# Float32 scores for items 8 to 15, a third VectorE pass for w1 and w2, and a DMA for q's second copy

## The chip, the cores and the metric

The kernel runs on one core of a Trainium2 chip. The metric is the device time of one execution in microseconds, lower is better. The engines named below are TensorE (PE; PEld is its weight load), VectorE (DVE), ScalarE (ACT), GpSimd (POOL) and SyncE (SP), which here issues all DMAs.

## The reference

Three stages run one after the other on 4 x 576 = 2304 tokens: an attention with 32 heads of 64, causal, whose scores have a decay added; a gated block (two products multiplied, then w3 and w_out); and a soft mixture of 8 experts with 4 slots each. What matters here:

```python
scores = scale * np.matmul(q, k.transpose(0, 1, 3, 2))
bias = -(cum[:, :, :, None] - cum[:, :, None, :])        # cum: running sum of max(s, 0)
scores = np.where(causal, -1000000000.0, scores + np.minimum(bias, 0.0))
...
attn = attn / (np.sum(attn, axis=-1, keepdims=True) + 1e-09)
x = attn @ v
a = x @ w1
b = x @ w2
h = a * b @ w3
x = h @ w_out
```

w1, w2, w3 and w_out reach the kernel as 64-bit floating point words, which it turns into float32 itself.

## The kernel before

**Items.** The attention is cut into 40 items (ITEMS). Items 0 to 7 are heads 0 to 7 with query tiles 0 to 2 (320 queries); items 8 to 15 are the same heads with tiles 3 and 4 (256 queries against 448 and 576 keys); items 16 to 39 are heads 8 to 31 with all five tiles. A step of the loop in att_steps does, for item n, its scores (att_scores), the scaling of item n-1 by its row sums (att_norm), the preparation of item n+1 (att_prep), the fetch of item n+2 (att_fetch), the transposes of item n-1 (att_transpose) and, for every second n, the product with v (att_pv).

**Scores, two ways.** Items below NF32 (8 before) multiply float32 operands: the raw tile holds q and k on 64 partitions and the decay rows on four more, and L323 multiplies 68 partitions of it; each such product is two TensorE instructions. Later items take float32r operands: the raw tile is fetched with q and k on both halves of the partitions (128), VectorE rounds q and k into qa (L295, L298), q's rounded copy goes into qb (L297, on ScalarE for n < 24 and on VectorE after), GpSimd subtracts to get the remainder of k in qb (L299) and of q in qa (L302), and L323 makes two products, with qa (128 partitions) and with qb (68).

**Tiles.** raw, qa and qb have two buffers each. A raw tile is free for the next fetch when its last reader is done: the casts and subtractions for a float32r item, the score matmuls themselves for a float32 item.

**Weights.** w1 and w2 come as 16 pieces of 512 words (k = 0 to 15 in load_words). convert makes float32 of one: ScalarE scales the high word (L182) and turns the low word into its shifted integer (L185); VectorE shifts and joins (L186) and puts the sign in (L189). Then ScalarE rounds it into the stationary operand (L205) and GpSimd subtracts to get the remainder (L206). w3 and w_out go through convert too, in two layouts.

**Order.** SP's instructions (all DMA issues) run in the order of the program. The other engines are ordered by a planner with its own costs, from the dependencies and the order of the program. The program weaves the attention's steps, the gated block's halves (glu_half, L421) and the pieces of weights by hand (weave): pieces 0 to 7 go with the first nine items, pieces 8 to 15 and the first gated halves with the items after that, and later pieces of w3 and w_out with the rest.

Of the kernel before, what the change touches and what calls it, by code (L numbers as in the profile page):

```python
# [10 lines left out]
F32 = mybir.dt.float32  # L11
F32R = mybir.dt.float32r
I32 = mybir.dt.int32
U32 = mybir.dt.uint32
I64 = mybir.dt.int64
AF = mybir.ActivationFunctionType
ALU = mybir.AluOpType
# [30 lines left out]
def attn_glu_softmoe_kernel(  # L48
# [14 lines left out]
    nc = tc.nc  # L63
# [19 lines left out]

    NW, NRAW, NG4, NX, NE_ = 8, 3, 4, 6, 11
    NRW, SCB, PTB, QAB, VB = 2, 3, 2, 2, 2
    NF32, NDIR, ND = 8, 2, 1

    A1, CA, CB1, CB, GB1, GB, GC = 0.6, 8, 16, 26, 8, 16, 24

# [84 lines left out]
        nc.sync.dma_start(raw, {"w12": w12, "wo": wo, "w3": w3, "wot": wot, "w3t": w3t}[kind][i, :, 512 * e : 512 * e + 512])  # L174
        words[k] = raw

    def convert(k, w):
        raw = words.pop(k)
        pair = raw.bitcast(I32).rearrange("p (n t) -> p n t", t=2)
        hi, lo = pair[:, :, 1], pair[:, :, 0]  # L180
        wi, wu = w.bitcast(I32), w.bitcast(U32)
        nc.scalar.activation(out=w, in_=hi.bitcast(F32), func=AF.Copy, scale=F64_SCALE)  # L182

        lu = lo.bitcast(U32)
        nc.scalar.activation(out=lo, in_=lu, func=AF.Copy, scale=LO_SCALE, bias=-0.49999)  # L185
        nc.vector.scalar_tensor_tensor(  # L186
            out=wi, in0=wi, scalar=3, in1=lo, op0=ALU.logical_shift_left, op1=ALU.bitwise_or
        )
        return nc.vector.scalar_tensor_tensor(  # L189
            out=wi, in0=hi, scalar=-0x80000000, in1=wi, op0=ALU.bitwise_and, op1=ALU.bitwise_or  # L190
        )

    w12_t = [None] * FC
    rows_t, rows_w = {}, {}

    def load_words(k, ap):
        (kind, i), e = TODO[k // 2], k % 2
        span = slice(512 * e, 512 * e + 512)
        if kind == "w12":
            if e == 0:  # L200
                w12_t[i] = wp.tile([P, 2, 2, KC, P], F32R, tag="W", name=f"w12t_{i}", bufs=NW)
            w = gq.tile([P, 512], F32, tag="g4", name=f"w_{kind}_{i}_{e}", bufs=NG4)
            convert(k, w)
            th, tl = (w12_t[i][:, n].rearrange("p a k f -> p (a k f)")[:, span] for n in range(2))
            nc.scalar.copy(out=th, in_=w)  # L205
            nc.gpsimd.tensor_tensor(out=tl, in0=w, in1=th.bitcast(F32), op=ALU.subtract)  # L206
        elif k < 2 * N0:
            if e == 0:
                rows_t[kind, i] = gq.tile([P, FC, P], F32, tag="g4", name=f"{kind}_{i}", bufs=NG4)
            rows_w[kind, i] = convert(k, rows_t[kind, i].rearrange("p c f -> p (c f)")[:, span])  # L210
        else:
            if e == 0:
                rows_t[kind, i] = ap.tile([P, 1024], F32, tag="words", name=f"w_{kind}_{i}", bufs=NRAW)
            w = rows_t[kind, i]
            convert(k, w[:, span])
            if e == 1:
                nc.sync.dma_start({"wo": wo_d, "w3": w3_d}[kind][i], w)

# [53 lines left out]
    def att_prep(n, ap):  # L272
        h, tiles = ITEMS[n]
        t = hd[n]
        raw, q0, q1 = t["raw"], t["q0"], t["q1"]
        if h % 2:
            vt = ap.tile([P, 9, 2, D], F32, tag="v", name=f"v_{n}", bufs=VB)
            nv = 2 * tiles[-1] + 1
            nc.sync.dma_start(vt[:, :nv], v[h // 2, :, :nv])
            t["v"] = hd[n - 1]["v"] = vt  # L280
        if n < NF32:
            rows = raw
        else:
            rows = ap.tile([P, 2, S], F32R, tag="qb", name=f"qb_{n}", bufs=QAB)
            qa = ap.tile([P, 2, S], F32R, tag="qa", name=f"qa_{n}", bufs=QAB)
        if n < NDIR:
            for a in range(2):
                nc.sync.dma_start(rows[64 + 2 * a : 66 + 2 * a, :, :q1].bitcast(F32), dec[a][h : h + 1, :, :, :q1])
        else:
            nc.sync.dma_start(rows[64:68, :, :q1].bitcast(F32), rows_d[h].rearrange("a b n t -> (a b) n t")[:, :, :q1])  # L290
        if n < NF32:
            t["mul"] = [rows[:68]]
            return
        rq, rk, qb = raw[:, 0], raw[:, 1], rows
        nc.vector.tensor_copy(qa[:, 0, q0:q1], rq[:, q0:q1])  # L295

        (nc.scalar.copy if n < 24 else nc.vector.tensor_copy)(qb[0:64, 0, q0:q1], rq[0:64, q0:q1])  # L297
        nc.vector.tensor_copy(qa[:, 1, :q1], rk[:, :q1])  # L298
        nc.gpsimd.tensor_tensor(  # L299
            out=qb[0:64, 1, :q1], in0=rk[0:64, :q1], in1=qa[0:64, 1, :q1].bitcast(F32), op=ALU.subtract  # L300
        )
        nc.gpsimd.tensor_tensor(  # L302
            out=qa[64:, 0, q0:q1], in0=rq[64:, q0:q1], in1=qa[64:, 0, q0:q1].bitcast(F32), op=ALU.subtract
        )
        t["mul"] = [qa, qb[:68]]
# [314 lines left out]
    def att_steps(ap):  # L620

        groups = [[] for _ in range(B + 1)]
        N = len(ITEMS)
        for n in range(N + 1):
            tiles = ITEMS[n][1] if n < N else ()
            old = [i for i in ITEMS[n - 1][1] if i] if 0 < n <= N else []
            sc = [(0.2 + 0.3 * i, lambda i=i, n=n: att_scores(n, i, ap)) for i in tiles]
            tr = [(0.2 + 0.3 * i, lambda i=i, n=n: att_transpose(n - 1, i, ap)) for i in old]
            norm = [(0, lambda n=n: att_norm(n - 1))] if 0 < n <= N else []
            prep = [(0, lambda n=n: att_prep(n + 1, ap))] if n + 1 < N else []  # L630
            if n + 2 < N:
                prep += [(0, lambda n=n: att_fetch(n + 2, ap))]
            blks = [k for k in range(2) if BLK[k][2][0] in ITEMS[n - 1][1]]
            pv = [(1.4, lambda n=n, k=k: att_pv(n - 2, k)) for k in blks] if n > 0 and n % 2 == 0 else []
            groups[min(B, max(0, (n - 1) // H))] += [
                *sc[:1], *norm, *sc[1:2], *prep, *sc[2:3], *tr[:1], *sc[3:4], *tr[1:2], *sc[4:], *tr[2:], *pv
            ]
        return groups
# [78 lines left out]
    with tc.tile_pool(name="att", bufs=1) as ap:  # L717
# [11 lines left out]
            out=mask[:, S - P :], in_=mask[:, S - P :], pattern=[[-1, P]], base=0,  # L729
# [4 lines left out]
        att = att_steps(ap)  # L734
        decay_rows()
        att_prep(0, ap)
        for k in range(2, NRAW):
            fetch_words(k, ap)
# [13 lines left out]
        def load(k):  # L752
            i = k // 2 - 1
            if FC <= i < N0:
                (sum_rows if k % 2 else use_rows)(*TODO[i])
            if k < 2 * N0:
                load_words(k, ap)
            if k + NRAW < 2 * N0:
                fetch_words(k + NRAW, ap)

        def load_later(i):
            for e in range(2):
                fetch_words(2 * i + e, ap)
            for e in range(2):
                load_words(2 * i + e, ap)
# [10 lines left out]
        k = GC - GB  # L776
        steps = steps[GB:]
        run(weave(att[2], weave(steps[:k], prep[CB:]) + steps[k:]))
        for b in range(2, B):
            steps, late = glu_steps(b - 1, late)  # L780
            n = len(more) // (B - b)
# [70 lines left out]
    for a in range(0, 4, 2):  # L852
        zt_ps = psum("tp", f"zt_ps_{a}")
        for c in range(2):
            nc.tensor.transpose(zt_ps[:, c * P : (c + 1) * P], z_acc[:, (a + c) * P : (a + c + 1) * P], ident)
        nc.vector.tensor_reduce(
            out=zt[:, a : a + 2], in_=zt_ps[:, : 2 * P].rearrange("p (c t s) -> p c s t", t=2, s=2 * NS),
# [14 lines left out]
    for q in range(4):  # L872
        cols = slice(256 * q, 256 * q + 256)
        yps = psum(("acc", "sg")[q % 2], f"y_ps_{q}")
        for r in range(2):
            for j in range(4):
                f = 4 * r + j
# [10 lines left out]
    for r in range(2):  # L888
        for c in range(2):
            for j in range(4):  # L890
                f = 4 * r + j
# [94 lines left out]
    for c in range(2):  # L986
# [10 lines left out]
        for n in CH[c]:  # L997
            ot = big(OT[n_out], f"ot_{n_out}").rearrange("p (n d) -> p n d", d=256)[:, : 2 * n]
            for m in range(n):
                op = psum("sg", f"out_ps_{n_out}_{m}")  # L1000
                for e in range(2):
# [7 lines left out]
                    out=ot[:, 2 * m : 2 * m + 2].rearrange("p n d -> p (n d)"), in_=op  # L1009
# [54 lines left out]
```

## Time and profile before

| | us |
|---|---|
| median of 3 runs | 590.42 |
| lowest and highest | 587.47, 592.25 |
| profiled execution | 585.76 |
| its span, first to last instruction | 583.9 |
| TensorE busy in it | 527.3 |
| VectorE, ScalarE, GpSimd busy in it | 347.9, 323.8, 218.6 |

An engine's busy time is the time in which an instruction of it was under way; matmuls are pipelined and their ends are modelled, so a busy TensorE is not one at its peak. A profile tells for each group of instructions how long one takes, how long the engine stood idle before them, and what ended that idle time. The granted clock is the share of its full speed that TensorE was given.

### The profile page before, as it was taken

To read this page: it belongs to the slowest core of one execution; us is meant where nothing else is said; L and a number is where in the kernel's file an instruction comes from. 1 tells how busy PE (TensorE), PEld (TensorE's weight loads), DVE (VectorE), ACT (ScalarE), POOL (GpSimd) and SP (SyncE) were. 2 spreads that over 40 slices of the span, in tenths; PEclk is the share of its full clock that TensorE was granted. 3 is DMA by queue.
4 is the path that set the end of the run, shared out by engine and by line. 5 is a ranking of instruction groups with operands and counts; after the bars stand their busy time and mean duration, and the time that the engine had idled before them with its cause. 6 is when DMAs were issued, how large, how long until landed. Compare 5 with 4: busy or idle time off the path is not lost. (4 is left out here: it accounts for less than half of the span.)

```text
span 583.9 us, 11901 instructions
## 1 busy us (share of the span) xinstructions
PE 527.3 (90%) x4324; PEld 443.6 (76%) x4324; DVE 347.9 (60%) x989; ACT 323.8 (55%) x877; POOL 218.6 (37%) x260
## 2 busy tenths in 40 slices
PE   1878988998698999989999889999999999999994
PEld 1655967787587797978989779898988999843463
DVE  6548998698887477484686756566740311252532
ACT  5767876778767666655566557466833321321212
POOL 5447887445927445161364443523410000001000
PEclk9995889998989999989999999999999999999999
DMA  6556744777562333524545254464450996689947
GB/s 200 178 164 192 241 153 174 245 273 262 188 196 81 126 101 122 165 79 156 182 160 174 92 172 139 128 211 172 134 222 32 375 407 244 238 305 421 419 175 262
DMA packets 37881, 116.19 MB, mean 199 GB/s; under 512 B 3808, under 2 KB 10656, under 8 KB 34368
## 3 DMA queue, kind: packets, MB, share of 16 engines
q1 hardware_dynamic: 37824, 115.45, 56.4%
q8 instruction: 34, 0.56, 0.4%
q14 instruction: 23, 0.19, 0.1%
HBM read 103.81 MB, written 11.60 MB: 198 GB/s over the span
## 5 line engine op out<-in xcount | busy, mean ns | idle before, releaser
L421 PE MATMUL gl<-x,w12t 128*128 128x320 f32 (+1 forms) x1536 | 237.0, 304 | 7.7 <-DVE nmax L326 5.6
L421 PEld LDWEIGHTS gl<-x,w12t 128*128 128x128 f32 x1536 | 214.0, 192 | 16.0 <-DVE nmax L326 7.6
L344 POOL TENSOR_SCALAR sc<-sc,rinv 128x64 f32<-128x64 f32 (+4 forms) x160 | 93.5, 603 | 68.0 <-DVE rinv L341 46.6
L331 ACT ACTIVATE sc<-sc,nmax 128x64 f32<-128x64 f32 (+4 forms) x160 | 89.5, 561 | 48.2 <-DVE nmax L326 47.8
L302 POOL TENSOR_TENSOR qa<-raw,qa 64x576 fp32r<-64x576 f32 (+1 forms) x32 | 43.5, 1358 | 135.3 <-DVE qa L295 116.6
L326 DVE CUSTOM_DVE_ANT_0 sc<-sc_ps,mask 128x64 f32<-128x64 f32 (+4 forms) x160 | 64.6, 422 | 27.9 <-PE sc_ps L323 26.0
L359 PE MATMUL pt_ps<-ident,sc 128*128 128x128 f32 x320 | 57.9, 291 | 5.6 <-ACT pt L361 2.6
L361 ACT COPY pt<-pt_ps 128x128 f32<-128x128 f32 (+3 forms) x128 | 52.0, 422 | 16.9 <-PE pt_ps L359 10.1
L323 PE MATMUL sc_ps<-qa 128*128 128x448 f32 (+1 forms) x168 | 55.5, 347 | 4.3 <-DVE nmax L326 1.8
L323 PE MATMUL sc_ps<-qb 68*128 68x448 f32 (+1 forms) x168 | 51.0, 325 | 7.9 <-DMA qb<-rows_d 7.9
L299 POOL TENSOR_TENSOR qb<-raw,qa 64x576 fp32r<-64x576 f32 x32 | 52.8, 1651 | 4.8 <-issue 0.9
L359 PEld LDWEIGHTS pt_ps<-ident,sc 128*128 128x128 f32 x320 | 38.6, 146 | 18.4 <-issue 10.4
L110 PE MATMUL x_ps<-pt,v 128*64 128x256 f32 (+1 forms) x384 | 48.4, 368 | 0.1
L427 ACT COPY a<-gl 128x256 f32<-128x256 f32 (+1 forms) x64 | 25.5, 398 | 37.8 <-PE gl L421 35.5
L964 POOL MEMSET ht<- 128x1024 f32 x2 | 1.9, 954 | 107.4 <-DVE ew L867 99.0
L186 DVE SCALAR_TENSOR_TENSOR w_w<-w_w,raw_w 128x512 int32<-128x512 int32 x32 | 25.2, 787 | 26.5 <-ACT raw_w L185 26.0
L323 PEld LDWEIGHTS sc_ps<-qb 68*128 68x128 f32 x168 | 32.8, 201 | 8.9 <-issue 8.5
L323 PEld LDWEIGHTS sc_ps<-qa 128*128 128x128 f32 x168 | 32.9, 198 | 8.4 <-DVE nmax L326 3.0
L110 PEld LDWEIGHTS x_ps<-pt,v 128*64 128x64 f32 x384 | 33.8, 146 | 6.7 <-issue 1.3
L182 ACT ACTIVATE w_w<-raw_w 128x512 f32<-128x512 f32 x32 | 21.6, 675 | 24.4 <-DMA raw_w<-in_w 24.3
L594 ACT COPY gn<-gn_ps 128x512 f32<-128x512 f32 x40 | 22.7, 584 | 18.0 <-PE gn_ps L591 17.0
L409 DVE TENSOR_TENSOR x<-x_ps,x 128x320 fp32r<-128x320 f32 (+1 forms) x32 | 13.7, 448 | 29.4 <-ACT x L408 29.4
(181 smaller groups left out, 830.2 us busy)
## 6 DMA issues: line engine op xcount, KB each, us to landing
ew<-in_ew SPq DMA_DIRECT2D x27, 1024.0 KB
raw_w<-in_w SPq DMA_DIRECT2D x32, 512.0 KB
raw<-in_qk SPq DMA_DIRECT2D x24, 576.0 KB
v<-in_v SPq DMA_DIRECT2D x16, 576.0 KB
raw_w3t<-in_w3t SPq DMA_DIRECT2D x16, 512.0 KB
raw_wot<-in_wot SPq DMA_DIRECT2D x8, 512.0 KB
raw_wo<-in_wo SPq DMA_DIRECT2D x8, 512.0 KB
w_d<-w_w SPq DMA_DIRECT2D x8, 512.0 KB
```

The costliest lines, as they stand in the source:

```text
L110: mm = nc.tensor.matmul(out_, lhs, rhs, start=start, stop=stop)
L186: nc.vector.scalar_tensor_tensor(out=wi, in0=wi, scalar=3, in1=lo, op0=ALU.logical_shift_left, op1=ALU.bitwise_or)
L299: nc.gpsimd.tensor_tensor(out=qb[0:64, 1, :q1], in0=rk[0:64, :q1], in1=qa[0:64, 1, :q1].bitcast(F32), op=ALU.subtract)
L302: nc.gpsimd.tensor_tensor(out=qa[64:, 0, q0:q1], in0=rq[64:, q0:q1], in1=qa[64:, 0, q0:q1].bitcast(F32), op=ALU.subtract)
L323: nc.tensor.matmul(pp[:r, : z - a], x[:, 0, q0 : q0 + r], x[:, 1, a:z], start=x is mul[0], stop=x is mul[-1])
L326: nc.vector.tensor_tensor_reduce(out=sc[:r, a:z], in0=pp[:r, : z - a], in1=hd["mask"][:r, m0 : m0 + z - a], scale=-0.125, scalar=3.0e38 if ...
L331: nc.scalar.activation(out=sc[:r, :W], in_=sc[:r, :W], func=AF.Exp, bias=nmax[:r, i : i + 1], scale=-1.0, accum_out=rsum[:r, i : i + 1],)
L344: nc.gpsimd.tensor_scalar(out=sc, in0=sc, scalar1=rinv[:, i : i + 1], scalar2=1.0, op0=ALU.mult, op1=ALU.mult)
L359: nc.tensor.transpose(tp[:, j * P : (j + 1) * P], sc[:, j * P : (j + 1) * P], ident)
L361: t["turned", i] = nc.scalar.copy(out=pt[:, p0 : p0 + step * (i - 1) + 1 : step], in_=tp[:, : i * P].rearrange("p (j q) -> p j q", q=P))
L421: nc.tensor.matmul(acc[:, :nt], w12_t[fc][:, wi, n, kc], x_t[b, blk, kc][:, xi], start=k == 0, stop=k == 3 * KC - 1)
L427: nc.scalar.copy(out=a_sb[:, :nt], in_=acc[:, :nt])
```

## The change

Three edits. NF32 goes from 8 to 16, so items 8 to 15 fetch q and k on 64 partitions only, have no qa and qb, and their decay rows go into the raw tile. For w1 and w2 convert leaves the low word to VectorE: it shifts the scaled high word (one tensor operand), joins the sign, and joins the low word shifted right by 29; ScalarE's pass over the low word is gone there, and w3 and w_out keep it. For items 16 to 39 q's second copy is a DMA from qa to qb inside SBUF, issued by ScalarE after VectorE's rounding, in place of a cast from raw.

```diff
-    NF32, NDIR, ND = 8, 2, 1
+    NF32, NDIR, ND = 16, 2, 1
...
-    def convert(k, w):
+    def convert(k, w, by_act):
...
         nc.scalar.activation(out=w, in_=hi.bitcast(F32), func=AF.Copy, scale=F64_SCALE)
-
         lu = lo.bitcast(U32)
+        if not by_act:
+            nc.vector.tensor_scalar(out=wi, in0=wi, scalar1=3, scalar2=None, op0=ALU.logical_shift_left)
+            nc.vector.scalar_tensor_tensor(
+                out=wi, in0=hi, scalar=-0x80000000, in1=wi, op0=ALU.bitwise_and, op1=ALU.bitwise_or
+            )
+            return nc.vector.scalar_tensor_tensor(
+                out=wu, in0=lu, scalar=29, in1=wu, op0=ALU.logical_shift_right, op1=ALU.bitwise_or
+            )
+
         nc.scalar.activation(out=lo, in_=lu, func=AF.Copy, scale=LO_SCALE, bias=-0.49999)
...
-            convert(k, w)
+            convert(k, w, False)
...
-            rows_w[kind, i] = convert(k, rows_t[kind, i].rearrange("p c f -> p (c f)")[:, span])
+            rows_w[kind, i] = convert(k, rows_t[kind, i].rearrange("p c f -> p (c f)")[:, span], True)
...
-            convert(k, w[:, span])
+            convert(k, w[:, span], True)
...
-        (nc.scalar.copy if n < 24 else nc.vector.tensor_copy)(qb[0:64, 0, q0:q1], rq[0:64, q0:q1])
+        nc.scalar.dma_start(qb[0:64, 0, q0:q1].bitcast(F32), qa[0:64, 0, q0:q1].bitcast(F32))
```

## Rows read from the trace of the kernel before

**Rows 1.** Stretches: length, busy us of PE, PEld, DVE, ACT, POOL, clock, DMA, GB/s.

```profile
36.00:47.40 11.40, 7.84 (x47) 5.26 (x47) 6.07 (x25) 7.41 (x23) 2.54 (x5) 0.77 0.74 227
47.40:63.00 15.60, 14.10 (x69) 10.92 (x69) 14.02 (x29) 11.21 (x34) 14.41 (x15) 0.51 0.72 232
63.00:97.30 34.30, 29.38 (x205) 26.68 (x201) 30.41 (x63) 26.36 (x61) 28.33 (x26) 0.95 0.56 191
...
140.00:200.00 60.00, 49.84 (x451) 43.27 (x452) 47.99 (x127) 42.92 (x119) 35.17 (x38) 0.91 0.52 176
200.00:440.00 240.00, 232.30 (x1941) 210.46 (x1940) 152.74 (x457) 145.70 (x414) 95.45 (x121) 0.99 0.44 148
```

**Rows 2.** Groups from 47 to 97 us: busy, mean ns, idle before.

```profile
L299 POOL TENSOR_TENSOR qb<-raw,qa 64x576 fp32r<-64x576 f32 x7 | 11.2, 1602 | 1.4 <-DMA raw_w<-in_w 0.5 <-PE pt_ps L359 0.5 <-ACT raw_w L185 0.4
L189 DVE SCALAR_TENSOR_TENSOR w_w<-raw_w,w_w 128x512 int32<-128x512 int32 x8 | 9.7, 1217 | 0.0
```

**Rows 3.** Single lines: count, shortest/median/longest ns, first and last start.

```profile
L185 ACT ACTIVATE raw_w<-raw_w x32: 637/661/737, 5.2 to 424.2; 128x512 int32<-128x512 uint32 x32
L186 DVE SCALAR_TENSOR_TENSOR w_w<-w_w,raw_w x32: 673/692/1900, 7.0 to 425.3; 128x512 int32<-128x512 int32 x32
L298 DVE CAST qa<-raw x32: 441/453/1684, 47.5 to 405.7; 128x576 fp32r<-128x576 f32 x32
L297 ACT CAST qb<-raw x16: 387/538/680, 47.4 to 182.3; 64x256 fp32r<-64x256 f32 x8, 64x576 fp32r<-64x576 f32 x8
L297 DVE CAST qb<-raw x16: 446/1670/1705, 196.4 to 406.1; 64x576 fp32r<-64x576 f32 x16
```

**Rows 4.** TensorE's groups by shape, 47.4 to 63 and 63 to 97.3 us.

```profile
L359 PE MATMUL pt_ps<-ident,sc 128*128 128x128 f32 x8 | 2.9, 436 | 1.1 <-ACT ptd L375 1.1
...
L421 PE MATMUL gl<-x,w12t 128*128 128x320 f32 x99 | 17.9, 333 | 4.9 <-DVE nmax L326 4.9
```

**Rows 5.** Timeline near 30 us: start, us, engine, instruction, idle before.

```profile
29.40 0.66 ACT L185 ACTIVATE raw_w<-raw_w 128x512 int32<-128x512 uint32 x1
...
30.30 0.37 PE L110 MATMUL x_ps<-ptd,v 128*64 128x64 f32 x1 [0.85 <-ACT ptd L375]
```

**Rows 6.** Timeline of TensorE's scores, with float32 (raw) and float32r (qa, qb).

```profile
35.83 1.32 PE L323 MATMUL sc_ps<-raw 68*128 68x64 f32 x6 [0.25 <-issue]
...
43.45 2.47 PE L323 MATMUL sc_ps<-raw 68*128 68x64 f32 x6 [0.47 <-DMA raw<-rows_d]
...
49.61 1.22 PE L323 MATMUL sc_ps<-qa 128*128 128x448 f32 x3 [1.32 <-POOL qa L302]
...
80.73 0.29 PE L323 MATMUL sc_ps<-qa 128*128 128x288 f32 x1
...
81.14 0.30 PE L323 MATMUL sc_ps<-qb 68*128 68x288 f32 x1
...
87.89 0.50 PE L323 MATMUL sc_ps<-qa 128*128 128x448 f32 x2
```

**Rows 7.** Timeline of a small transfer and its reader; SP's issues of L290, shortest/median/longest.

```profile
6.37 1.58 SPq L288 DMA_DIRECT2D raw<-rows  x2
...
9.22 2.47 PE L323 MATMUL sc_ps<-raw 68*128 68x64 f32 x6 [9.22 <-DMA raw<-rows]
...
L290 SPq DMA_DIRECT2D qb<-rows_d x32: 267/327/742, 42.0 to 405.2; - x32
```

**Rows 8.** Timeline of item 16: cast, second subtraction, first reduction.

```profile
108.87 0.46 DVE L295 CAST qa<-raw 128x576 fp32r<-128x576 f32 x1 [1.90 <-DMA raw<-in_qk]
...
111.06 1.42 POOL L299 TENSOR_TENSOR qb<-raw,qa 64x576 fp32r<-64x576 f32 x1
...
118.55 0.23 DVE L326 CUSTOM_DVE_ANT_0 sc<-sc_ps,mask 128x64 f32<-128x64 f32 x1 [0.30 <-PE sc_ps L323]
```

**Rows 9.** TensorE's waits, 200 to 440 us: us in total, times, longest.

```profile
PE lg L110 <- DVE nmax L326: 2.1, 1, 2.1
```

**Rows 10.** What ended ScalarE's idle time before L297: us, times.

```profile
  DMA raw<-in_qk: 5.0, 4
```

## The prediction

> **What bounds the kernel now.** I read the page's busy shares and its row of clocks first, then a table of stretches, then the groups of instructions inside the stretch that the change touches, and last the waits of each engine.
>
> The table of stretches splits the kernel into three [rows 1]. From 200 to 440 us TensorE is busy 232.3 of 240 us and nothing else comes near: the stretch is TensorE's, and what VectorE or ScalarE saves there is worth only the little that TensorE waits for them. From 140 to 200 us no engine is full: TensorE is busy 49.8 of 60. The stretch from 36 to 97.3 us is where items 8 to 15 have their scores. There three engines are nearly full together: from 47.4 to 63 us TensorE 14.1, VectorE 14.0 and GpSimd 14.4 of 15.6 us, and TensorE is granted 0.51 of its clock, which is its lower level, 1.2 GHz, for nearly all of it. From 63 to 97.3 us they are busy 29.4, 30.4 and 28.3 of 34.3 us.
>
> The groups inside this stretch show that VectorE's load is partly not its own [rows 2]: the second bitwise pass over a word takes 1.22 us on average here while GpSimd runs 1.60 us subtractions beside it, and the first pass, of the same shape, has a median of 0.69 over the kernel [rows 3]. TensorE's own idle time is 4.9 us for VectorE's score reduction and 1.1 for a ScalarE copy [rows 4].
>
> **Part by part.** The sum is made against the profiled execution (span 583.9 us, time 585.76, so 1.9 us lie outside the span). The runs shown have their median 4.7 us higher, at 590.42; I carry the difference over unchanged.
>
> *w1 and w2, words 0 to 7 (before 47 us).* ScalarE loses one 0.66 us pass for each word [rows 3], VectorE gains a shift. The trace has no integer shift with one tensor operand. Its bounds are the plain cast of 128x576, 0.45 us, and the two-operand pass of the same shape, 0.69; a shift has one tensor operand like the cast, so I take 0.45. What the ScalarE pass is worth is seen at 29.4 us: it runs, the copy of ptd starts only behind it, and TensorE waits 0.85 us for that copy [rows 5]. If all eight passes stood so, 8 x 0.66 = 5.3 us would come back; if all eight shifts stood on the path, 8 x 0.69 = 5.5 us would be lost. VectorE is the emptier of the two here, busy 6.1 of 11.4 us against ScalarE's 7.4 from 36 us on [rows 1]. I take -1.0 us.
>
> *Items 8 to 15 and words 8 to 15 (36 to 97.3 us).* Taken away for each item: VectorE's two casts, ScalarE's cast, and GpSimd's two subtractions, of which the long one alone is 1.60 us [rows 2]. TensorE pays. Six instructions over 576 columns of float32 operands took 1.32 us behind other matmuls and 2.47 us at 43.45 us, after gaps [rows 6]; the two are a factor of 1.9 apart, as the two levels of the clock are. Per column that is 2.29 and 4.29 ns, so an item of 448 + 576 columns costs 2.35 or 4.39 us. The float32r items cost, at the higher level, 0.71 us for the four matmuls of 288 columns (80.73 to 81.44) and 0.50 for the two of 448, together 1.21; at the lower, 1.22 for the three with qa and as much again for the same columns with qb, 2.44 us [rows 6]. The difference is +1.14 us or +1.95 us for an item. With three items at the lower level (8 to 10, before 63 us) and five at the higher: 3 x 1.95 + 5 x 1.14 = 11.6 us; bounds 9.1 and 15.6.
>
> The Trainium skill, "FP8 and Floating Point Precision", TensorE Precision Notes, says that true FP32 takes four passes through the array. As an estimate by that page, at 2.4 GHz against two single passes, an item would cost 0.85 us more and all eight 6.8; the rows say 9.1 at that level, and the sum goes by the rows.
>
> What comes back: item 8's scores start at 49.61 us, when GpSimd's result is there, though item 7's ended at 43.45 + 2.47 = 45.92, so 3.7 us; the 4.9 us and 1.1 us of [rows 4]; the lower clock from 63 us on, 5% of 34.3 = 1.7 us; and the gated products that follow item 7 come about 3.2 us earlier, since items 8 and 9 no longer put their two 1.60 us subtractions in front of item 7's scaling on GpSimd, and with them the higher clock, which is worth half, 1.6. That is 13.0 us against 11.6, so -1.4 us. Bounds: +11.6 if nothing comes back. At the other end TensorE's lost capacity from 36 to 97.3 us is 3.6 + 1.5 + 4.9 us idle and 2.6 + 7.6 + 1.7 us at the lower level [rows 1], 21.9 us, less 9.1: -12.8.
>
> Where cover is needed: a float32 item reads its raw tile directly, so the fetch of the item after next waits on SP for TensorE's scores and no longer for GpSimd, and behind it on SP stand the weight words, v and the decay rows. The tile is needed two items later, and eight items fill the 50 us from 47.4 to 97.3, so two take 12 us, against 4.4 us of scores and about 3 of landing [rows 6, 7]; I cost it at nothing. If this cover goes, each fetch costs what its landing takes, about 3 us. The fetch also halves (64 partitions), which helps. VectorE's eight added shifts (8 x 0.45 = 3.6 us) take the place of its eight casts of k (0.45 us plain, [rows 3]), so the casts of q and ScalarE's eight passes over the low word are the gain.
>
> *q's copy, items 16 to 23 (97 to 200 us).* ScalarE's cast (0.68 us at the longest, [rows 3]) becomes a DMA that it issues. The trace has no copy inside SBUF; the nearest row is a small transfer: issued at 6.37, awaited by TensorE until 9.22, 2.85 us [rows 7]. It starts when VectorE's cast is done: for item 16 at 109.33, so it lands at about 112.5 with 0.33 us for the issue (SP's median for a transfer of this kind, [rows 7]), and GpSimd's second subtraction, needed by the same matmuls, ends at 112.48. VectorE's first reduction of item 16 starts at 118.55, so some 6 us cover both [rows 8]. 0 us; bounds -5.4 (8 x 0.68, all of ScalarE's cast on the path) and +2.6 (8 x 0.33). Without the cover it would be 2.85 us for an item.
>
> *q's copy, items 24 to 39 (200 to 440 us).* VectorE loses 16 casts with a median of 1.67 us, though the shortest took 0.45 [rows 3]. TensorE waits for VectorE in five rows here, 2.1 us the largest and 3.9 in all [rows 9]. I take half, -2.0 us; bounds -3.9 and +5.3 (16 issues of 0.33 us on ScalarE).
>
> Sum: -1.0 - 1.4 + 0 - 2.0 = -4.4 us: 581.4 for an execution like the profiled one, 586.0 at the median.
>
> **The rivals.**
>
> *The relief carries.* TensorE closes most of its gaps from 36 to 97.3 us and stays at the higher clock. For it: VectorE and GpSimd are both above 85% there and both are cut. Against: TensorE is as full. Near -10 us in that stretch (the bound is -12.8), -1 and -3 around it, is 14 less than the median: 576 us.
>
> *The hold passes on.* VectorE's long casts are long because GpSimd is working beside them: 0.45 us at the shortest, 1.67 at the median [rows 3]. If the next VectorE instruction is held in the cast's place, nothing is won from 200 us on, and half of the 4.9 us stays in the middle: -1.0 + (2.4 - 1.4) + 0 + 0 = 0, so 590 us. The Trainium skill, "SBUF — State Buffer", Who interferes with whom, says just this: a VectorE copy, or an operation with two SBUF inputs, and GpSimd lock each other out of a shared port pair for a whole instruction. The bitwise passes at 1.22 us agree.
>
> *ScalarE's queue is held (slower).* An issue waits for VectorE's cast, and in order behind it on ScalarE stand exp, the copies of pt, ptd and of the gate, for which TensorE waits. Before, ScalarE's cast waited only for the raw data, and even so 5.0 us over four of sixteen [rows 10]; from item 24 on ScalarE had no such wait. At 0.33 us of issue and 0.4 of hold, the 16 items from 24 on cost 11.7 us if TensorE gets all of it: 590.4 - 4.4 + 11.7 = 598 us. It decides, that is, brings the time above 590.4, from 4.4 / 16 = 0.28 us for each of them on, and makes it slower by 1% at 0.64. Against it: ScalarE is busy 145.7 of 240 us there, so a hold can be hidden.
>
> **How the numbers follow.** Forecast 0.40 (580 to 592), relief carries 0.17, hold passes on 0.17, queue held 0.26. A measurement of this kernel can tell about 1% from no change: below 584.5 is faster, above 596.3 slower. Faster: 0.17 and 0.18 of the forecast's, 0.35. Same: 0.22 of the forecast's and 0.15 of the third, 0.37. Slower: 0.26 and 0.02, 0.28. The range of 576 to 600 leaves out about half of the carried relief (0.08), a third of the held queue (0.08) and the ends of unknown costs (0.04).
>
> **What would show it.** Item 8's scores near 46 us and without a GpSimd wait; eight float32 items at 2.4 us, at most three of them at 4.4; items 8 to 15 ending between 93 and 99 us; no row of a pass over w1 or w2 at 0.66 us more on ScalarE, and a VectorE shift near 0.45; ScalarE's idle time in front of the copies' issues below 0.3 us each; TensorE's idle time from 200 to 440 us two us shorter. I am wrong if the lower clock lasts beyond 63 us (each further us costs half of one), if the float32 items come closer together than TensorE can take them, or if the planner, which orders all engines but SP by its own costs, puts the work from 97 us on in a worse order.

## The result, and the profile after

The changed kernel takes 579.4 us in the median of four runs (577.37 to 580.04); the kernel before, run beside it, 588.94 (587.31 to 592.25). The ratio is 0.9875, with a 95% interval of 0.9837 to 0.9912: faster, clear of noise though by less than 2%, by 9.5 us in the medians and 7.4 by the ratio. Here and below the medians are over all runs, the ratios and their intervals over the fast ones alone (up to 1.5% above the kernel's fastest), so the two need not agree. The time is inside the range of 576 to 600 and below the 584.5 that the prediction put as the edge of "faster", an outcome it gave 0.35; the forecast of 586.0 was 6.6 us too high, of which 1.5 lie in the baseline (588.94 here, 590.42 there). Against the baseline of its own comparison the forecast was a ratio of 0.9925 (586.0 / 590.42). The largest term of its sum, -2.0 us for q's copy from 200 us on, is not where the gain is.

The profiled execution has a span of 576.9 us (before 583.9). Its stretches, as [rows 1] (stretch and length, busy us of PE, PEld, DVE, ACT and POOL with counts, granted clock, DMA share, GB/s):

```profile
36.00:47.40 11.40, 9.55 (x71) 7.29 (x72) 7.58 (x30) 8.35 (x28) 3.42 (x5) 0.91 0.70 218
47.40:63.00 15.60, 15.01 (x59) 10.69 (x58) 13.30 (x34) 10.88 (x27) 10.81 (x13) 0.63 0.62 203
63.00:97.30 34.30, 33.22 (x234) 26.68 (x231) 24.29 (x63) 22.80 (x55) 13.19 (x15) 1.00 0.64 205
97.30:140.00 42.70, 36.29 (x270) 30.35 (x268) 33.46 (x73) 26.57 (x65) 16.53 (x16) 0.88 0.68 217
140.00:200.00 60.00, 55.49 (x522) 47.34 (x521) 46.50 (x130) 44.52 (x130) 39.56 (x43) 0.97 0.55 175
200.00:440.00 240.00, 233.87 (x1956) 212.89 (x1955) 141.47 (x436) 143.99 (x405) 89.64 (x115) 0.99 0.49 158
```

From 36 to 47.4 us TensorE is busy 9.55 us where it was 7.84. From 63 to 97.3 us it is busy 33.22 of 34.3 us (29.38) at a granted clock of 1.00 (0.95), while VectorE has fallen from 30.41 to 24.29 and GpSimd from 28.33 to 13.19. Up to 97.3 us TensorE has run 364 matmuls in these rows, 71 + 59 + 234, against 321 in the three of before. From 97.3 to 140 us it falls back: 36.29 us busy at a granted clock of 0.88, where the kernel before has, in a stretch that [rows 1] leave out:

```profile
97.30:140.00 42.70, 39.43 (x342) 33.20 (x340) 33.99 (x85) 31.47 (x79) 21.10 (x19) 1.00 0.67 225
```

From 140 to 200 us TensorE goes from 49.84 to 55.49, and from 200 to 440 us from 232.30 to 233.87.

TensorE's timeline of the changed kernel, scores of items 8, 9 and 13 from float32 operands (start, us, count last):

```profile
46.65 3.78 PE L330 MATMUL sc_ps<-raw 68*128 68x448 f32 x6
...
52.81 3.69 PE L330 MATMUL sc_ps<-raw 68*128 68x448 f32 x6
...
84.91 1.89 PE L330 MATMUL sc_ps<-raw 68*128 68x448 f32 x6
```

TensorE's waits in the changed kernel from 36 to 97.3 us (us in total, times, longest):

```profile
PE sc_ps L330 <- DVE w_w L189: 1.2, 1, 1.2
...
PE pt_ps L366 <- ACT ptd L382: 0.6, 1, 0.6
PE gl L428 <- DVE nmax L333: 0.3, 1, 0.3
```

The 4.9 us for VectorE's reduction of [rows 4] are down to 0.3, and GpSimd's 1.3 us in front of item 8 [rows 6] are gone.

The other place that changed is near 155 us. TensorE's largest wait there in the kernel before, from 140 to 200 us:

```profile
PE sc_ps L323 <- DMA qb<-rows_d: 7.1, 2, 5.8
```

SP's timeline there, also before (start, us, issues):

```profile
142.40 12.54 SPq L174 DMA_DIRECT2D raw_w3t<-in_w3t  x4
154.99 0.33 SPq L290 DMA_DIRECT2D qb<-rows_d  x1
```

The decay rows of an item stood on SP behind four pieces of w3, whose buffers VectorE had not freed, and TensorE stood idle for 5.8 us. The changed kernel has no wait for decay rows there. Following the gated products (L421 before, L428 after), the 97th starts at 95.1 us before and 94.8 after, the 241st at 150.7 and 154.3, the 289th at 184.0 and 178.4, the last at 510.9 and 503.8: by this mark no lead at 97 us, a lead of 5.6 at 184, and 7.1 at the end.

The mark follows one kind of product, and the order among the kinds changed too. By 97.3 us both kernels have begun 90 score matmuls, but of all others the changed kernel has begun 343 and the kernel before 298: 22 more products with v, 12 more transposes, 8 more products with w_out and 3 more gated ones. At the median distances between starts of such matmuls in these traces that is some 3.6 us of TensorE's time, an estimate. So there is a lead at 97 us; in these two executions it is lost by 140 us (579 others begun, 604 before), over a stretch in which the changed kernel has the lower clock, and is there again at 184 (903 and 845).

### The profile page after: what moved, and what is told of

Read it like the earlier page. It is cut to its first block, busy times and chain, and to the rows that moved or that the text cites. A ratio compares the mean times of both kernels' runs of the same rounds, so it can differ in the third digit from the quotient of the medians.

```text
span 576.9 us, 11909 instructions
## 1 busy us (share of the span) xinstructions
PE 529.7 (92%) x4324; PEld 442.1 (77%) x4324; DVE 329.8 (57%) x973; ACT 311.1 (54%) x845; POOL 195.5 (34%) x244
## 5 line engine op out<-in xcount | busy, mean ns | idle before, releaser
L428 PE MATMUL gl<-x,w12t 128*128 128x320 f32 (+1 forms) x1536 | 241.7, 308 | 3.9 <-DVE nmax L333 2.0
L428 PEld LDWEIGHTS gl<-x,w12t 128*128 128x128 f32 x1536 | 216.2, 194 | 12.6 <-DVE nmax L333 3.7
L351 POOL TENSOR_SCALAR sc<-sc,rinv 128x64 f32<-128x64 f32 (+4 forms) x160 | 90.8, 585 | 62.4 <-DVE rinv L348 47.6
L309 POOL TENSOR_TENSOR qa<-raw,qa 64x576 fp32r<-64x576 f32 x24 | 36.8, 1535 | 146.5 <-DVE qa L303 141.2
L330 PE MATMUL sc_ps<-qa 128*128 128x64 f32 (+1 forms) x144 | 46.6, 336 | 6.7 <-DVE nmax L333 2.8
L366 PEld LDWEIGHTS pt_ps<-ident,sc 128*128 128x128 f32 x320 | 40.4, 149 | 15.8 <-issue 7.1
L330 PE MATMUL sc_ps<-raw 68*128 68x288 f32 (+4 forms) x96 | 35.7, 517 | 16.6 <-DMA raw<-rows 12.8
L330 PE MATMUL sc_ps<-qb 68*128 68x64 f32 (+1 forms) x144 | 44.0, 309 | 0.9 <-issue 0.9
L306 POOL TENSOR_TENSOR qb<-raw,qa 64x576 fp32r<-64x576 f32 x24 | 37.8, 1574 | 2.2 <-issue 0.5
L330 PEld LDWEIGHTS sc_ps<-raw 68*128 68x128 f32 x96 | 20.3, 250 | 23.0 <-issue 13.9
L330 PEld LDWEIGHTS sc_ps<-qa 128*128 128x128 f32 x144 | 27.7, 193 | 10.4 <-DVE nmax L333 4.5
L347 DVE TENSOR_SCALAR rinv<-rsum 128x5 f32<-128x5 f32 (+2 forms) x40 | 25.4, 636 | 10.7 <-ACT sc L338 10.5
```

What stands on the lines that cost most here:

```text
L306: nc.gpsimd.tensor_tensor(out=qb[0:64, 1, :q1], in0=rk[0:64, :q1], in1=qa[0:64, 1, :q1].bitcast(F32), op=ALU.subtract)
L309: nc.gpsimd.tensor_tensor(out=qa[64:, 0, q0:q1], in0=rq[64:, q0:q1], in1=qa[64:, 0, q0:q1].bitcast(F32), op=ALU.subtract)
L330: nc.tensor.matmul(pp[:r, : z - a], x[:, 0, q0 : q0 + r], x[:, 1, a:z], start=x is mul[0], stop=x is mul[-1])
L347: nc.vector.tensor_scalar(out=rinv[:, span], in0=t["rsum"][:, span], scalar1=EPS, scalar2=None, op0=ALU.add)
L351: nc.gpsimd.tensor_scalar(out=sc, in0=sc, scalar1=rinv[:, i : i + 1], scalar2=1.0, op0=ALU.mult, op1=ALU.mult)
L366: nc.tensor.transpose(tp[:, j * P : (j + 1) * P], sc[:, j * P : (j + 1) * P], ident)
```

## The experiments

The first eight are the edits one by one and in pairs, with two kernels for a rival that this reading suggested: that the gain is the missing wait for decay rows and not the relief of VectorE and GpSimd. The last four ask which engine's relief it is, and whether more items would bring more. Every ratio is to the kernel before, run on the same chip.

**Float32 operands for items 8 to 15, alone.**

```diff
-    NF32, NDIR, ND = 8, 2, 1
+    NF32, NDIR, ND = 16, 2, 1
```

> Items 8 to 15 by float32 operands alone; w1, w2 and q's copy as before. Theory 1 (the gain is made where those items stand: VectorE and GpSimd relieved, TensorE paying): most of the 7 us, -4 to -7 us, with x of items 8 to 11 some 10 us earlier. Theory 2 (the gain is the 5.8 and 1.3 us that TensorE waited for decay rows near 155 and 174 us, whose fetches stand on SP behind weight words): -5 to -7 only if that wait is gone in its trace too, else 0 +-2 us. The forecast's sum without the other two edits: about 0 (11.6 against 13.0, of which some 1.1 is ScalarE's).

579.66 against 585.73 us; 0.9858 [0.9815, 0.9901]. The edit alone gives as much as the whole change. No wait for decay rows is left in its trace from 97 to 200 us, so this run alone does not tell the two theories apart.

**Three VectorE passes for w1 and w2, alone.**

```diff
+        if not by_act:
+            nc.vector.tensor_scalar(out=wi, in0=wi, scalar1=3, scalar2=None, op0=ALU.logical_shift_left)
...
-            convert(k, w)
+            convert(k, w, False)
```

> w1 and w2 by three VectorE passes alone. The forecast's sum: -1 us from words 0 to 7, and in the full stretch of words 8 to 15 VectorE, which is full there, gets 8 x 0.43 us more: so -1 to +3 us. Theory 2: 0 unless the wait near 155 us changes.

595.02 against 585.73; 1.0155 [1.0126, 1.0184]. Alone it is a loss, of 9 us. Its stretch from 47.4 to 63 us, to be read beside that of [rows 1] and of the changed kernel:

```profile
47.40:63.00 15.60, 8.87 (x35) 7.03 (x34) 15.56 (x30) 8.19 (x21) 13.61 (x16) 0.72 0.61 195
```

VectorE, which was busy 14.02 of the 15.6 us before, is now busy 15.56, and TensorE's busy time there falls from 14.10 to 8.87 (35 matmuls for 69); in the changed kernel, with sixteen float32 items, the two engines are at 13.30 and 15.01. In this trace the third pass stands where VectorE had no room for it.

**q's second copy by DMA, alone** (with eight float32 items it is 32 copies).

```diff
-        (nc.scalar.copy if n < 24 else nc.vector.tensor_copy)(qb[0:64, 0, q0:q1], rq[0:64, q0:q1])
+        nc.scalar.dma_start(qb[0:64, 0, q0:q1].bitcast(F32), qa[0:64, 0, q0:q1].bitcast(F32))
```

> q's second copy by DMA alone, here for items 8 to 39, so also in the full stretch. The forecast's sum: -2 us from 200 us on. The rival of ScalarE's queue: +5 to +12 us. Theory 2: 0 +-2, or -5 to -7 if the wait near 155 us is gone.

585.15 against 585.73; 0.9995 [0.9968, 1.0022]: nothing. From 140 to 200 us its trace has 0.5 us of the 7.1 us of waiting for decay rows left, so that wait went here without a gain, which speaks against theory 2.

**The kernel before, with the decay rows of items from 16 on issued by ScalarE's queue.** It takes away what put them behind the weights.

```diff
-            nc.sync.dma_start(rows[64:68, :, :q1].bitcast(F32), ...)
+            (nc.scalar if n >= 16 else nc.sync).dma_start(rows[64:68, :, :q1].bitcast(F32), ...)
```

> The kernel before with one edit of another kind: from item 16 on the decay rows are fetched by ScalarE's queue, not by SP's, so they no longer stand behind weight words. Theory 1: the wait of 5.8 us goes, but it was not what the change removed; 0 to -3 us as TensorE falls into the next wait. Theory 2: -5 to -7 us, the whole gain of the change without any of its edits. If ScalarE's queue holds things up by 24 issues of 0.33 to 0.47 us: up to +5.

584.39 against 585.73; 0.9967 [0.9939, 0.9994]. TensorE's waits from 140 to 200 us in it:

```profile
PE sc_ps L323 <- DVE nmax L326: 2.9, 3, 1.7
PE gl L421 <- DVE nmax L326: 2.4, 3, 1.0
PE ptd_ps L373 <- ACT pt L361: 1.4, 2, 0.8
PE pt_ps L359 <- POOL sc L344: 0.7, 2, 0.5
```

The 7.1 us for decay rows are gone from this stretch, but the waits for VectorE, ScalarE and GpSimd come to 7.7 us with a last one of 0.3, where they were 3.4 before; of the 5.8 us or more that this rival needs, 2 are gained. The rival falls as the explanation of the whole: without the wait at 155 us other waits stand in its place.

**The pairs**, and the changed kernel with the same move of the decay rows. Each is the changed kernel or before with the diffs shown above.

> The changed kernel without the DMA: q's copy for items 16 to 39 by ScalarE (n under 24) and VectorE, as before. If the DMA brings the forecast's 2 us from 200 us on, this loses 2 of the 7: -5 us. If the DMA brings nothing, -7; if ScalarE's queue was held, better than -7.

582.88 against 588.09; 0.9878 [0.9807, 0.9949].

> The changed kernel without the third VectorE pass: w1 and w2 as before. If that edit brings the forecast's 1 us or more, -6 us or less; if it costs, better than -7.

588.34 against 588.09; 0.9971 [0.9929, 1.0014].

> The changed kernel with items 8 to 15 by float32r as before (q's copy of them by DMA as well). Theory 1: the gain is mostly gone, 0 to -3 us. Theory 2: what the wait near 155 us does decides.

585.66 against 588.09; 0.9970 [0.9941, 0.9999].

> The changed kernel with the decay rows of items 16 to 39 fetched by ScalarE's queue. Theory 2: the wait is gone already, so no more than -1 us over the changed kernel's -7. Theory 1: any wait for the rows that it still has goes too; -7 to -10 against the kernel before.

586.25 against 588.09; 0.9974 [0.9937, 1.001]. A move that was worth 0.3% on the kernel before takes 1% away from the changed one.

The eight combinations of the three edits in one table, as the change of the time in %:

| | neither | w1, w2 | DMA copy | both |
|---|---|---|---|---|
| eight float32 items | 0 | +1.55 | -0.05 | -0.30 |
| sixteen | -1.42 | -1.22 | -0.29 | -1.25 |

Sixteen items are better by 1.42, 2.77, 0.24 and 0.95 in the four columns, on average 1.35% (7.9 us); the 0.24 lies within the intervals and is not told from none. The other two edits average +0.13% and -0.2% over their four pairs, and each has both signs. The effects do not add: each interval is some 0.3 to 0.7 to either side, and the difference between the columns is larger than that.

The traces show a lead where these items stand. Matmuls other than scores that TensorE has begun by 97.3 us, with eight and with sixteen float32 items: 298 and 309, 284 and 321 (with w1 and w2), 288 and 331 (with the DMA copy), 294 and 343 (with both), and each time as many score matmuls or more. What is left of it at the end differs: beside the DMA copy hardly any.

**GpSimd's work put back into the changed kernel.** For items 8 to 15 it again does two subtractions of the old sizes, into a tile that nobody reads.

```diff
+            if n >= 8:
+                xa = ap.tile([P, 2, S], F32R, tag="qa", name=f"xa_{n}", bufs=QAB)
+                nc.gpsimd.tensor_tensor(
+                    out=xa[0:64, 0, q0:q1], in0=raw[0:64, 0, q0:q1], in1=raw[0:64, 0, q0:q1], op=ALU.subtract
+                )
+                nc.gpsimd.tensor_tensor(
+                    out=xa[0:64, 1, :q1], in0=raw[0:64, 1, :q1], in1=raw[0:64, 1, :q1], op=ALU.subtract
+                )
```

> The changed kernel, but for each of items 8 to 15 GpSimd again does its two subtractions (64 x 256 and 64 x 576 columns, as in the kernel before) from the landed query tile into a tile that nobody reads; scores still come from the float32 operands, so the result is the same. It puts GpSimd's 3.2 us per item back and nothing else; no product waits for them. If the gain is the relief of GpSimd's column (its own work and what it holds on VectorE), most of it goes: 584 to 588 us, +4 to +8 over the changed kernel. If it is the relief of VectorE, or that the products no longer wait for converted operands, little goes: 579 to 582.

586.08 against 585.52; 1.0013 [0.998, 1.0045]. The whole gain is gone, though the scores are still made from float32 operands and wait for nobody's conversion. The subtractions put back take 0.77 and 1.21 us on average, 15.8 in all, where the kernel before had 0.92 and 1.60. VectorE's three passes over the words from 47.4 to 97.3 us in the changed kernel (busy us, mean ns):

```profile
L186 DVE SCALAR_TENSOR_TENSOR w_w<-raw_w,w_w 128x512 int32<-128x512 int32 x8 | 7.6, 951 | 0.1
L189 DVE SCALAR_TENSOR_TENSOR w_w<-raw_w,w_w 128x512 uint32<-128x512 uint32 x8 | 6.1, 767 | 0.0
...
L185 DVE TENSOR_SCALAR w_w<-w_w 128x512 int32<-128x512 int32 x8 | 3.8, 480 | 3.1 <-ACT w_w L182 3.1
```

The same groups in this kernel:

```profile
L186 DVE SCALAR_TENSOR_TENSOR w_w<-raw_w,w_w 128x512 int32<-128x512 int32 x8 | 11.5, 1442 | 0.1
L189 DVE SCALAR_TENSOR_TENSOR w_w<-raw_w,w_w 128x512 uint32<-128x512 uint32 x9 | 7.9, 877 | 0.1
L185 DVE TENSOR_SCALAR w_w<-w_w 128x512 int32<-128x512 int32 x8 | 6.0, 749 | 3.5 <-ACT w_w L182 3.5
```

VectorE's instructions are the same ones, and the three take 0.49, 0.11 and 0.27 us more each, in the order of the rows, with GpSimd's subtractions put back. The Trainium skill, "SBUF — State Buffer", Who interferes with whom, says that GpSimd and such VectorE instructions lock each other out of a shared port pair; these rows agree.

This kernel's stretches need care:

```profile
36.00:47.40 11.40, 11.06 (x47) 8.01 (x45) 5.86 (x24) 7.59 (x26) 2.72 (x5) 0.50 0.59 187
47.40:63.00 15.60, 15.44 (x54) 10.48 (x53) 13.55 (x29) 8.85 (x22) 13.99 (x17) 0.50 0.69 216
63.00:97.30 34.30, 31.10 (x180) 26.61 (x179) 23.94 (x48) 18.08 (x44) 20.03 (x21) 0.80 0.41 134
```

In the profiled execution TensorE's clock fell to the lower level at 35.5 us, before the first added subtraction, and stayed there for 30.7 us; by the 97th gated product it was 10.9 us behind the changed kernel. Ten of the other executions had a mean clock of 0.968, where the changed kernel's four had 0.972, and their mean is 585.9 us. So the loss does not hang on that clock, but in which place of an ordinary execution it stands these rows cannot show. Nor can the run part GpSimd's work from the new order that the planner gives each edit: the moved decay rows above, which add no work to GpSimd or VectorE, took 1.0% from the changed kernel where this takes 1.38%.

**VectorE's two casts put back instead.**

```diff
+            if n >= 8:
+                xa = ap.tile([P, 2, S], F32R, tag="qa", name=f"xa_{n}", bufs=QAB)
+                nc.vector.tensor_copy(xa[0:64, 0, q0:q1], raw[0:64, 0, q0:q1])
+                nc.vector.tensor_copy(xa[0:64, 1, :q1], raw[0:64, 1, :q1])
```

> The changed kernel, but for each of items 8 to 15 VectorE again does the two casts of the landed query tile (0.45 us or so each where nothing holds it, 1.5 us beside GpSimd) into a tile that nobody reads. It puts VectorE's share of the removed work back and leaves GpSimd relieved and the products free of the wait. If VectorE's relief carries the gain: 583 to 587 us. If GpSimd's does, or the missing wait of the products: 579 to 582. If neither this nor the run with GpSimd's work back loses 2 us or more, the gain is in what the products no longer wait for.

581.98 against 585.52; 0.9941 [0.9906, 0.9975]. About half of the gain is gone, 0.66% of 1.25, though the two intervals just touch, and 581.98 lies at the upper end of the case in which VectorE's relief does not carry the gain. The casts took 0.45 and 0.79 us on average, 9.9 us of VectorE in all. Putting back GpSimd's work costs 1.38% and VectorE's 0.66%, together more than the gain, so these do not add either; but neither leaves the gain whole, and GpSimd's is the larger. Matmuls other than scores begun by 97.3 us follow the same order: 343 in the changed kernel, 326 here, 272 with GpSimd's work back. In both kernels the fetch into raw waits again for the added readers, so that each puts back this hold too.

**Twenty and twenty-four float32 items.**

```diff
-    NF32, NDIR, ND = 16, 2, 1
+    NF32, NDIR, ND = 20, 2, 1
```

> The changed kernel with twenty items by float32 operands instead of sixteen. Items 16 to 19 take some 0.9 to 1.4 us more of TensorE each (from the float32 products of the changed kernel's trace, 2.05 us against 1.21 for two tiles of 448 and four of 288 columns), and give back VectorE's and GpSimd's work for each. If TensorE has slack in that stretch and the others set the pace, as where items 8 to 15 stand: 575 to 578 us. If TensorE sets the pace from there on: 580 to 585 us, the price of 4 to 6 us standing whole.

> The changed kernel with twenty-four items by float32 operands. Same two readings, twice the size: 572 to 577 us if VectorE and GpSimd set the pace for items 16 to 23, 583 to 591 if TensorE does. If twenty items gain and twenty-four lose, the pace passes to TensorE between them.

583.16 and 576.94 against 585.52; 0.9933 [0.9897, 0.9969] and 0.9831 [0.977, 0.9892]. Twenty items are no better than sixteen, and twenty-four are not told apart from sixteen, whose interval reaches from 0.9837 to 0.9912. Neither reading, pace by VectorE and GpSimd or pace by TensorE, predicts such an order. The stretches with twenty-four:

```profile
97.30:140.00 42.70, 41.81 (x332) 34.26 (x325) 26.52 (x84) 30.79 (x79) 6.17 (x12) 1.00 0.60 188
140.00:200.00 60.00, 57.22 (x499) 46.93 (x499) 36.22 (x116) 42.40 (x123) 20.72 (x32) 0.97 0.50 150
```

TensorE is busy 99.0 of these 102.7 us where the changed kernel has 91.8, VectorE falls by 17.2 us and GpSimd by 29.2: with items 16 to 23 taken over too, TensorE is nearly full here.

## Why the prediction was right or wrong

**Words 0 to 7, -1.0 us: not confirmed.** The shift takes what was taken for it:

```profile
L185 DVE TENSOR_SCALAR w_w<-w_w x16: 408/426/775, 6.8 to 80.3; 128x512 int32<-128x512 int32 x16
```

0.43 us against 0.45. But the worth of the edit is between -1% and +1.6% by what stands beside it, +0.13% on average. That it costs 9 us alone was not among the prediction's cases, whose lower and upper bounds were -5.3 and +5.5. In that kernel eight float32r items still load VectorE from 47 us on, where words 8 to 15 add their shifts, and there the trace has VectorE full and TensorE less busy, as shown above. Beside the other two edits it is worth -0.96%. Why the DMA copy, which takes no VectorE work away before item 24, mends all of it (+1.55 to -0.30%) is open.

**Items 8 to 15, -1.4 us: the mechanism borne out as far as it was tested, the term mis-sized.** This edit is the whole gain: 1.35% on average, 7.9 us, 8.3 alone by the ratio. That the sum came out in its range all the same is in part luck: this term was some 6.5 us too small, and the -1.0 and -2.0 beside it are not confirmed. Three parts of the step can be told apart.

The price of TensorE was too high. An item takes 1.89 us, or 2.05 where it stands split at 69.90 and 72.64 us (2.22 in three pieces, item 10), against 1.21 before, +0.68 to +0.84 (+1.01) where +1.14 was taken; at the lower level 3.78 and 3.69 against 2.44, +1.3 where +1.95 was taken; and two items stand there, not three. That is 2 x 1.3 + 6 x 0.76 = 7.2 us, not 11.6. The failed step is the scaling of 2.29 and 4.29 ns per column from groups of six small products [rows 6], whose time does not all grow with the columns. In the changed kernel's trace the instructions of an unsplit item start 0.38 us apart for 448 columns and 0.24 for 288, both 0.84 ns per column, and the last one ends 0.16 us after the next could have started. In the small group the 64-column instructions start 0.11 to 0.13 us apart, where 0.84 ns a column would give 0.05. So of its 1.32 us some 0.97 (2 x 576 x 0.84 ns) go by columns, and the rest, the end of the last instruction and the excess of the small ones, was multiplied too. The Trainium skill, "FP8 and Floating Point Precision", TensorE Precision Notes, by which the prediction estimated 0.85 us for an item and 6.8 for eight, comes nearer than the rows that were scaled: the trace has 0.68 to 1.01 for an item at the higher level.

What comes back near the place was forecast well: item 8's scores start at 46.65 us (forecast 46, before 49.61), the wait for VectorE's reduction falls by 4.6 of 4.9 us, the clock from 63 us on is 1.00. With the right price the step would have said 7.2 - 13.0 = -5.8 us, and the sum 581.6, a ratio of 0.9851.

At 97.3 us, where the sum closed its account, the gated products show nothing of this: item 14's scores start at 92.15 us against 93.52, and the 97th gated product is 0.3 us earlier. The lead stands in the 45 other matmuls counted above, some 3.6 us where the corrected step has 5.8, and shows next in item 15. The prediction let the eight items end at 97.3 us; before, item 15's scores end at 109.5, and in the changed kernel at 103.0, 6.5 us earlier. Further behind, VectorE's first pass over a word of w3 came forward. In the timeline of the changed kernel:

```profile
114.95 1.96 DVE L194 SCALAR_TENSOR_TENSOR w3t<-w3t,raw_w3t 128x512 int32<-128x512 int32 x1
```

and in that of the kernel before:

```profile
125.80 0.68 DVE L186 SCALAR_TENSOR_TENSOR w3t<-w3t,raw_w3t 128x512 int32<-128x512 int32 x1
```

Counted from the 97th gated product, so that a slower start falls out, that pass begins:

| kernel | us after the 97th gated product |
|---|---|
| before, decay rows on ScalarE's queue | 30.7, 30.8 |
| w1 and w2; DMA copy; both | 26.2, 28.1, 28.2 |
| changed; with decay rows on ScalarE's queue | 20.2, 19.4 |
| sixteen items alone; with w1 and w2; with DMA copy | 21.2, 20.0, 21.2 |
| changed with GpSimd's or VectorE's work back | 20.9, 21.0 |
| twenty, twenty-four items | 19.4, 16.6 |

In the pairs that differ by the sixteen items alone the weights come 6 to 10 us nearer: 30.7 to 21.2, 26.2 to 20.0, 28.1 to 21.2, 28.2 to 20.2. That it becomes TensorE's time between 150 and 184 us, where before stood idle, is seen in the changed kernel's trace and is not shown to be the cause: the kernel with sixteen items and the DMA copy has 21.2 us and yet gains only 0.29%, and with GpSimd's work put back the weights stand as near, at 20.9, and nothing is gained. What became of the lead behind 97 us is open in detail.

**q's copy, items 16 to 39, 0 and -2.0 us: nothing that can be told from none.** The edit alone is -0.05%, -0.2% on average. The issue takes more than was taken (count, shortest, median and longest ns):

```profile
L304 ACTq EVENT_SEMAPHORE  x29: 17/38/2443, 126.8 to 397.4; - x29
L304 ACTq DMA_DIRECT2D qb<-qa x24: 468/468/513, 99.3 to 397.6; - x24
```

0.47 us where SP's 0.33 [rows 7] was assumed; with ScalarE busy 144 of 240 us from 200 us on, no cost is seen. From the 289th gated product to the last the lead grows from 5.6 to 7.1 us in the one pair of traces, which goes the forecast's way by 1.5 us.

**The rivals.** *The relief carries* agrees best with the runs: GpSimd's and VectorE's work put back takes all or half of the gain away. A new order of the planner can be worth nearly as much, as said above, so this is not fully shown. Its size, 14 us by nearly the whole of TensorE's gaps, was too much. *The hold passes on* is half right. From 200 to 440 us 21.9 us of VectorE's casts went away (15 casts of 1.46 us), and its busy time fell by 11.3, from 152.74 to 141.47. Two of the groups that took their place, from 200 to 440 us in the changed kernel (busy us, mean ns):

```profile
L194 DVE SCALAR_TENSOR_TENSOR w_w<-w_w,raw_w 128x512 int32<-128x512 int32 x16 | 14.2, 890 | 11.9 <-ACT raw_w L193 11.9
...
L347 DVE TENSOR_SCALAR rinv<-rsum 128x5 f32<-128x5 f32 x17 | 12.5, 734 | 7.3 <-ACT sc L338 7.1
```

and before:

```profile
L186 DVE SCALAR_TENSOR_TENSOR w_w<-w_w,raw_w 128x512 int32<-128x512 int32 x16 | 11.5, 721 | 17.3 <-ACT raw_w L185 17.2
...
L340 DVE TENSOR_SCALAR rinv<-rsum 128x5 f32<-128x5 f32 x17 | 6.9, 409 | 3.9 <-ACT sc L331 3.7
```

The same instructions take 0.17 and 0.33 us more each. From 47 to 97 us it did so less: there GpSimd's own work went too, and the second two-operand pass takes 0.77 us where it took 1.22 [rows 2]. The first one hardly gains, 0.95 us against 0.98 in the kernel before:

```profile
L186 DVE SCALAR_TENSOR_TENSOR w_w<-w_w,raw_w 128x512 int32<-128x512 int32 x8 | 7.9, 982 | 0.5 <-ACT raw_w L185 0.5
```

*ScalarE's queue is held* did not come. The waits in front of the issues have a median of 0.038 us, one of them 2.4, where the rival took 0.4. With 0.47 for the issue that is still 0.51 us for each, above the 0.28 from which the rival was to decide, but only if TensorE loses all of it, and the edit alone costs nothing that can be told from noise.

**What was to show it.** Item 8 near 46 us without GpSimd: yes. Items at 2.4 and at most three at 4.4 us: fewer and cheaper. Items 8 to 15 ending between 93 and 99 us: no, at 103.0. TensorE's idle time from 200 to 440 us two us shorter: 1.6, by its busy time. The planner's order, named as what could make it wrong, is the likely source of what does not add: that is argued, since the plan itself was not varied.

## What to carry to other kernels

Where several engines are nearly full together, moving a step onto TensorE can pay by what it takes off the others, the held time of their neighbours included. A lead is to be looked for in all of an engine's work: one kind of product as the mark, here the gated ones, showed none at 97 us, where other matmuls had one. A price for a larger product is taken from a group of its own size, or from the distances between the starts of its instructions. And when an order is planned anew with each edit, an edit's worth measured alone says little of its worth in company: one edit here was +1.6% alone and -1.0% beside the other two.

## What the runs showed of the hardware

An integer shift of 128x512 takes VectorE 0.43 us in the median of 16, which the trace of before had no row for. The issue of a DMA by ScalarE took 0.468 us in the median of 24 and 0.513 at the longest.

TensorE's lower clock level begins at another time in each of the three kernels' traces (35.5, 42.3 and 45.3 us), and seems to cost less than the prediction charged. Over the 23, 28 and 29 executions of the kernel before in three comparisons, a further microsecond at the lower level, as worked out from each one's mean granted clock and span, went with 0.19, 0.12 and 0.11 us of time, not with the half that the prediction charged. The standard errors are 0.04 to 0.05, and it is a correlation across executions, not a test.
